# A load stream's ring in SBUF moved from 32 bytes past a 2 KB boundary onto the boundary

## The chip, the cores and the metric

The kernel runs on one core of one Trainium2 chip. The metric is the device time of one execution in microseconds (us), as a median of several executions. Where a ratio is given, it is the ratio of the runs of two kernels, taken in the same rounds, so it is not quite the ratio of the medians that are quoted beside it.

Two terms are used throughout. A *packet* is one record of the trace's list of DMA transfers: in this kernel mostly one contiguous run of bytes of one partition, moved by one of the 16 DMA engines. A *beat* is the time of 32 bytes in one DMA engine. The trace's packets give 27.2 bytes per ns per engine (below), so a beat is 1.176 ns.

## The reference, cut to what matters

One decoder step for a batch of 8: modulation from a condition, layer norm, attention of one new query against a long cache (32 query heads, 4 key/value heads, 8192 keys of 128 numbers), then a gated feed-forward block.

```python
mod = (_silu(c) @ w_mod).reshape(c.shape[0], 6, 1, -1)          # w_mod 1024 x 6144
h = _layernorm(x) * (1 + ca) + sa
q = h @ wq                                                      # 1024 x 4096
scores = einsum('bhqd,bhkd->bhqk', q, k) * Dh ** (-0.5)         # k_cache 8 x 4 x 8192 x 128
o = einsum('bhqk,bhkd->bhqd', softmax(scores), v)               # v_cache 8 x 4 x 8192 x 128
x = x + ga * (o @ wo)                                           # 4096 x 1024
h = _layernorm(x) * (1 + cb) + sb
x = x + gb * ((relu(h @ W_gate) * (h @ W_up)) @ W_down)         # 1024 x 3584, twice, and 3584 x 1024
```

With one query per batch entry there is little arithmetic for each byte. Of the 185.63 MB that are read from memory, 134 MB are K and V.

## The kernel before

All weights and all of K and V pass through one ring buffer in SBUF, `arena`, of nine slots of 16 KB per partition. A load is issued by the sync engine as soon as the ring space that it overwrites has been read.

```python
SLOT = 8192
NSLOT = 9
...
rem = nc.sbuf_base % 2048
if rem:
    sb("pad", [128, (2048 - rem) // 2], dt.bfloat16)
arena = sb("arena", [128, NSLOT * SLOT], dt.bfloat16)
ktb = sb("kt", [128, 2 * SLOT], dt.bfloat16)
... # some thirty small tiles
def pump():
    while stream:
        key, src, n = stream[0]
        lo = cursor[0] if cursor[0] + n <= NSLOT * SLOT else 0
        if P.unread("arena", lo, lo + n):
            return
        ...
        dst = arena[:, lo:lo + n]
        if len(src.shape) == 3:
            dst = dst.rearrange("p (a n) -> p a n", a=src.shape[1])
        P.op("sp", lambda e, dst=dst, src=src: e.dma_start(dst, src), writes=[slot_r(lo, lo + n)], dma=True)
```

The streamed tensors differ in how long their contiguous runs are. A K or V block gives each partition one run of 16,384 bytes. The rows of W_o are runs of 2,048 bytes.

```python
for n in range(N):                                              # N = 32
    load(("k", n), A_k_cache[n // G, n % G].rearrange("(p c) d -> p (c d)", p=128), SLOT)
    load(("v", n), A_v_cache[n // G, n % G].rearrange("(p c) d -> p (c d)", p=128), SLOT)
wo_src = A_wo.rearrange("(q h d) n -> q d h n", q=4, d=128)
```

The padding was meant to place the ring on a 2 KB boundary. But `nc.sbuf_base` is 16,481 when this kernel is built, and the allocator rounds each tile's start up to a multiple of 32. The pad of 1,950 bytes therefore began at 16,512, and the ring began at 18,464, which is 32 bytes past 18,432 = 9 x 2048. All blocks of the ring and all runs in it are multiples of 2 KB long, so every packet of the stream was written to an address 32 bytes past a 2 KB boundary.

## Time and profile before

| | before |
|---|---|
| median of 3 runs | 451.89 us (451.32 to 451.95) |
| span of the profiled run | 450.1 us |
| DMA packets of the stream's queue | 98.2% of 16 engines' span |
| PE, DVE busy | 67%, 48% |

The page of the kernel before, cut to the rows of the 40 slices that matter (busy share in tenths, granted clock in tenths, GB/s moved), the DMA queues (packets, MB, share of the 16 engines' span) and the chain of work that ended last:

```profile
span 450.1 us, 7822 instructions
...
PE   0234464678777775775897677688687768557853
...
PEclk9985566966888869679668887866768888655555
DMA  8999999999999999999999999999999999999992
GB/s 348 406 431 430 422 432 430 419 428 428 422 427 428 424 425 430 422 427 431 419 428 427 422 430 424 428 427 422 430 424 422 431 403 385 407 428 421 422 419 115
...
q1 hardware_dynamic: 16704, 185.64, 98.2%
q8 instruction: 27, 0.44, 0.4%
...
DMA 83%; PE 8%; DVE 7%; issue 1%; ACT 0%; SPq 0%; POOL 0%; DVEq 0%; ACTq 0%; POOLq 0%
```

The DMA row is at its highest digit almost from end to end, while PE is never at its own for long. From its third slice to the last but one, the GB/s row stays at 419 to 432, except in three slices of 403, 385 and 407, where the 2 KB rows of W_o arrive. So the kernel is as long as its stream, plus a few microseconds at each end.

The groups that read the ring or K^T, and the issues of the K loads (KB each, median us from issue to landing), from the same page:

```profile
L411 DVE STREAM_TRANSPOSE kt<-arena 128x1024 uint32<-128x1024 uint32 x128 | 153.3, 1219 | 117.1 <-DMA arena<-in_A_k_cache_dram 117.1
L420 PE MATMUL ps<-kt,qpad 128*128 128x512 bf16 x512 | 170.6, 503 | 2.0 <-POOL qpad L400 2.0
...
arena<-in_A_k_cache_dram SPq DMA_DIRECT2D x32, 2048.0 KB, 26.9
```

The transposes of K idle 117.1 us waiting for K data: the engines wait for the stream. A load lands 26.9 us after its issue, though 2 MB take only about 5 us at 427 GB/s, so some five loads are always queued, and it is the packets, not the issue of loads, that set the pace.

### The profile page before, as it was taken

How to read it: one execution, taken by the hardware profiler on the slowest of the kernel's cores; microseconds unless marked ns; L12 is line 12 of the kernel's file. 1: busy time of each engine (PE TensorE's matmuls, PEld its weight loads, DVE VectorE, ACT ScalarE, POOL GpSimd, SP SyncE). 2: the span in 40 equal slices, each digit the busy share in tenths (PEclk: the TensorE clock that was granted, in tenths of full speed). 3: DMA queues.
4: the chain of work that ended last, by engine and by line, in shares of the span. 5: the costliest groups of instructions: out<-in, count | busy, mean ns of one | idle time of the engine just before them, and what ended most of it. 6: DMA issues, size and time to landing. Idle time of an engine off the chain costs nothing.

```text
span 450.1 us, 7822 instructions
## 1 busy us (share of the span) xinstructions
PE 300.6 (67%) x3514; PEld 168.2 (37%) x3514; DVE 217.7 (48%) x333; ACT 33.2 (7%) x78; POOL 31.0 (7%) x141
## 2 busy tenths in 40 slices
PE   0234464678777775775897677688687768557853
PEld 0111121344433333343443344344343434447741
DVE  0503064666665566566555666655556663230000
ACT  0200020000010000000100000010000002000000
POOL 4000020100000001000000100000001000000000
PEclk9985566966888869679668887866768888655555
DMA  8999999999999999999999999999999999999992
GB/s 348 406 431 430 422 432 430 419 428 428 422 427 428 424 425 430 422 427 431 419 428 427 422 430 424 428 427 422 430 424 422 431 403 385 407 428 421 422 419 115
DMA packets 16769, 186.14 MB, mean 414 GB/s; under 512 B 1536, under 2 KB 1632, under 8 KB 5984
## 3 DMA queue, kind: packets, MB, share of 16 engines
q1 hardware_dynamic: 16704, 185.64, 98.2%
q8 instruction: 27, 0.44, 0.4%
q14 instruction: 6, 0.05, 0.0%
q10 hardware_dynamic: 32, 0.01, 0.0%
HBM read 185.63 MB, written 0.02 MB: 412 GB/s over the span
## 4 chain that ended last, share of the span: by engine, by line
DMA 83%; PE 8%; DVE 7%; issue 1%; ACT 0%; SPq 0%; POOL 0%; DVEq 0%; ACTq 0%; POOLq 0%
DMA arena<-in_A_k_cache_dram 61%; DMA arena<-in_B_W_down_dram 8%; DMA arena<-in_A_wq_dram 7%; DMA arena<-in_A_wo_dram 4%; PE ps L460 4%; DVE kt L411 3%; DMA c_r<-in_c_dram 2%; PE ps L528 1%; DVE pT L450 1%; PE ps L334 1%; PE ps L357 0%; PE ps L509 0%; DVE lu L281 0%; PE ps L420 0%; ACT L278 0%
## 5 line engine op out<-in xcount | busy, mean ns | idle before, releaser
L411 DVE STREAM_TRANSPOSE kt<-arena 128x1024 uint32<-128x1024 uint32 x128 | 153.3, 1219 | 117.1 <-DMA arena<-in_A_k_cache_dram 117.1
L420 PE MATMUL ps<-kt,qpad 128*128 128x512 bf16 x512 | 170.6, 503 | 2.0 <-POOL qpad L400 2.0
L420 PEld LDWEIGHTS ps<-kt,qpad 128*128 128x128 bf16 x512 | 63.5, 124 | 98.8 <-issue 72.6
L460 PE MATMUL ps<-pT,arena 128*128 128x8 bf16 x2048 | 56.0, 166 | 43.5 <-DVE pT L450 43.4
L460 PEld LDWEIGHTS ps<-pT,arena 128*128 128x128 bf16 x2048 | 54.0, 96 | 57.9 <-issue 57.6
L400 POOL COPY qpad<-qR 32x32 bf16<-32x32 bf16 x128 | 26.2, 205 | 316.4 <-PE ps L420 258.1
L430 PE MATMUL ps<-identf,negm 128*128 128x128 f32 x64 | 21.6, 433 | 36.5 <-DVE negm L426 36.5
L444 ACT ACTIVATE prb<-ps,bias 128x512 bf16<-128x512 f32 x32 | 22.0, 687 | 287.4 <-DVE mjt L438 287.4
L528 PE MATMUL ps<-hT,arena 128*128 128x8 bf16 x448 | 24.8, 194 | 8.4 <-DMA arena<-in_B_W_gate_dram 3.8
L430 PEld LDWEIGHTS ps<-identf,negm 128*128 128x128 f32 x64 | 13.5, 262 | 39.8 <-DVE negm L426 39.8
L528 PEld LDWEIGHTS ps<-hT,arena 128*128 128x128 bf16 x448 | 24.4, 152 | 8.9 <-DMA arena<-in_B_W_gate_dram 3.9
L450 DVE STREAM_TRANSPOSE pT<-prb 128x512 bf16<-128x512 bf16 x32 | 21.5, 672 | 1.7 <-ACT prb L444 1.7
L426 DVE TENSOR_REDUCE negm<-ps 128x1 f32<-128x512 f32 x32 | 20.9, 653 | 2.6 <-PE ps L420 2.6
L357 PE MATMUL ps<-arena,hT 128*32 128x512 bf16 x64 | 7.6, 627 | 12.5 <-DMA arena<-in_A_wq_dram 9.6
L535 DVE TENSOR_TENSOR hmT<-ps,grel 128x224 bf16<-128x224 f32 x1 | 0.4, 392 | 31.4 <-ACT grel L533 31.4
L303 PE MATMUL ps<-st,sel 128*128 128x1 f32 x4 | 1.2, 362 | 19.4 <-DVE st L302 19.4
L334 PE MATMUL ps<-arena,hT 128*32 128x512 bf16 x96 | 8.7, 528 | 7.2 <-DMA arena<-in_w_mod_dram 7.2
L545 PE MATMUL ps<-arena,hmT 128*32 128x256 bf16 x112 | 7.1, 415 | 7.5 <-DMA arena<-in_B_W_down_dram 7.4
L509 PE MATMUL ps<-arena,oT 128*32 128x256 bf16 x128 | 6.0, 366 | 5.1 <-DVE oT L497 2.6
L341 DVE COPY mod<-ps 128x512 f32<-128x512 f32 x2 | 1.3, 670 | 15.3 <-PE ps L334 15.3
L357 PEld LDWEIGHTS ps<-arena,hT 128*32 128x32 bf16 x64 | 1.9, 128 | 18.2 <-DMA arena<-in_A_wq_dram 16.1
L436 DVE TENSOR_REDUCE mj<-ps 128x8 f32<-128x128 f32 x32 | 8.1, 253 | 1.2 <-PE ps L430 1.2
(64 smaller groups left out, 64.6 us busy)
## 6 DMA issues: line engine op xcount, KB each, us to landing
arena<-in_A_k_cache_dram SPq DMA_DIRECT2D x32, 2048.0 KB, 26.9
arena<-in_A_v_cache_dram SPq DMA_DIRECT2D x32, 2048.0 KB, 30.4
arena<-in_w_mod_dram SPq DMA_DIRECT2D x4, 3072.0 KB, 18.3
arena<-in_A_wq_dram SPq DMA_DIRECT2D x4, 2048.0 KB, 35.9
arena<-in_A_wo_dram SPq DMA_DIRECT2D x4, 2048.0 KB, 19.7
arena<-in_B_W_gate_dram SPq DMA_DIRECT2D x4, 1792.0 KB, 25.8
arena<-in_B_W_up_dram SPq DMA_DIRECT2D x4, 1792.0 KB, 28.6
arena<-in_B_W_down_dram SPq DMA_DIRECT2D x3, 1792.0 KB, 34.4
```

The source lines that it names most:

```text
L334: fns.append(lambda e, w=w, pr=pr, j=j, kk=kk: e.matmul(ps[32 * j:32 * j + 32, pr, :], hT[:, kk, :], w[:, 2 * pr:2 * pr + 2, j, :], start= ...
L357: fns.append(lambda e, w=w, z=z, g=g, kk=kk: e.matmul(ps[32 * g:32 * g + 32, 3 + z, :], hT[:, kk, :], w[:, g, z, :], start=(kk == 0), stop ...
L400: P.op("pool", lambda e, n=n, Q=Q: e.tensor_copy(qpad[32 * Q:32 * Q + 32, n % NQ, :, 24 + 32 * Q:32 + 32 * Q], qR[32 * Q:32 * Q + 32, :, n ...
L411: P.op("dve", lambda e: e.transpose(ktb[:, to:to + QE].bitcast(dt.uint32), arena[:, lo:lo + QE].bitcast(dt.uint32)), reads=[slot_r(lo, lo ...
L420: fns.append(lambda e, t=t, r=r: e.matmul(ps[:, n % 2, :].rearrange("p (c k) -> p c k", k=32), qpad[:, n % NQ, t * 2 + r, 24 - 8 * i:152 - ...
L426: P.op("dve", lambda e: e.tensor_reduce(negm[:, n % 2:n % 2 + 1], ps[:, n % 2, :], AX.X, ALU.max, negate=True), reads=[bank(n % 2)], write ...
L430: P.op("pe", lambda e: e.matmul(ps[:, 2, 0:128], negm[:, n % 2:n % 2 + 1].to_broadcast([128, 128]), identf[:], start=True, stop=True), rea ...
L436: P.op("dve", lambda e: e.tensor_reduce(mj[:, z, :], ps[:, 2, 0:128].rearrange("p (m j) -> p j m", j=J), AX.X, ALU.min), reads=[bank(2)], ...
L444: P.op("act", lambda e: e.activation(prb[:, z, :], ps[:, z, :], ACT.Exp, bias=bias[:, z:z + 1], scale=scale, accum_out=lall[:, n:n + 1]), ...
L450: P.op("dve", lambda e: e.transpose(pT[:, z, :], prb[:, z, :]), reads=[R("prb", z, z + 1)], writes=[R("pT", z, z + 1)])
L460: fns.append(lambda e, cc=cc: e.matmul(ps[:, 3, col:col + J], vv[:, cc, :], pv_[:, cc % 16, cc // 16, :], start=(cc == 0), stop=(cc == NC ...
L528: fns.append(lambda e, w=w, f=f, kk=kk, off=off, first=first: e.matmul(ps[:, 0, off + f * B:off + (f + 1) * B], w[:, f // FR, f % FR, :], ...
```

## The change

The intent is to put the ring where the padding was meant to put it. Nothing else is edited. K^T and all small tiles move down by 32 bytes with it.

```diff
-        rem = nc.sbuf_base % 2048
+        rem = (nc.sbuf_base + 31) // 32 * 32 % 2048
         if rem:
             sb("pad", [128, (2048 - rem) // 2], dt.bfloat16)
         arena = sb("arena", [128, NSLOT * SLOT], dt.bfloat16)
```

## The prediction

> What bounds the kernel: the load stream. The DMA queue table gives its queue 98.2% of the 16 engines' span, and the 40 slices show the DMA busy share at 9 nearly throughout, at 419 to 432 GB/s. The chain of waits is 83% DMA, 8% PE, 7% DVE; no compute engine is busy over 67%. The sync queue waits for freed ring space, but a K load takes 26.9 us from issue to landing while 2 MB stream in about 5 us, so some five loads are always queued: the limit is how fast the engines move packets, not issue.
>
> What a packet costs. The trace's records of single packets (one contiguous run each) have these medians: 2,048 B 87 ns, 4,096 B 161, 8,192 B 313, 14,336 B 539, 16,384 B 614, 24,576 B 915. The slope from 2,048 to 16,384 B is 27.2 bytes per ns; left over at every size are 10 to 12 ns (minimum 8 to 9). So the byte rate is one fixed ceiling, and only the constant per packet is to be had. There are 15,104 data packets, 944 per engine: 944 x 11.6 ns = 11 us, an upper bound of 2.4% on a gain from alignment.
>
> What the change does. The allocator rounds to 32 bytes and the padding did not count that, so each destination run in the ring started 32 bytes past a 2 KB boundary. Now each starts on one (all blocks and rows are multiples of 2 KB). Nothing is added or removed; K^T and all small tiles move down by 32 bytes too, so relative addresses don't change. The Trainium skill ("DMA: Bandwidth & Descriptors", "How a descriptor splits into AXI transactions") says that a read not starting at a multiple of 256 B pays the 32 B beats before its start; whether a write pays, no run here shows. At 27.2 B/ns a beat is an estimated 1.18 ns, so each beat saved per packet is worth 944 x 1.18 = 1.1 us. A hint: two 8,192 B transfers of another queue took 307 ns, the stream's mostly 313: 2 to 5 beats, if their destinations were aligned, which I can't see. My central guess is 2 beats: 2.2 us. Nothing is nearly as likely; 5 beats would be 5.5 us.
>
> How much is critical. Nearly all: the last W_down data lands at 445.7 of 450.1 us, with 4 us of tail; PE is idle 20% or more of the K/V stage. The greatest relative effect should be on 2 KB rows (W_o, slices at 403 and 385 GB/s). I expect DVE, PE and ACT durations unchanged.
>
> Predicted: 449.6 us, range 445.5 to 452.3. Chances: faster by over 2% 0.06, within 2% 0.92, slower by over 2% 0.02.
>
> What would show it. Right: the median 16,384 B packet falls from 614 ns to 608-613, 2,048 B from 87 to 81-86, by the same ns at each size; steady K/V slices gain 0 to 4 GB/s; W_o slices rise most; transposes stay at 1,219 ns. Wrong: packets change in proportion to size, or packets unchanged while the span changes, or DVE/PE durations move.
>
> What would make it wrong. The constant may be entirely the unaligned start (then 441 us). Or a 2 KB boundary may make the partitions' writes meet in one place in some way this trace can't show, and packets get slower. Or a faster stream is eaten by ring space coming free late (then landings shorten while the SP queue's gaps grow).

## The result, and the profile after

| | before | after |
|---|---|---|
| median of 4 runs | 451.92 us (451.32 to 452.05) | 446.05 us (445.68 to 446.82) |
| ratio of the runs, 95% interval | | 0.9875 (0.9858 to 0.9892) |
| span of the profiled run | 450.1 us | 444.1 us |

The gain is 5.9 us, or 1.3%. The same cuts of the page of the kernel after:

```profile
span 444.1 us, 7822 instructions
...
PE   0235355677858676776877767786777787558753
...
PEclk9995576887788888879688888778888869655555
DMA  8999999999999999999999999999999999999993
GB/s 344 421 428 425 434 434 428 426 429 437 427 428 432 431 426 426 435 434 425 426 434 429 425 429 435 429 425 432 429 430 428 429 421 403 422 430 429 426 429 151
...
q1 hardware_dynamic: 16704, 185.64, 98.5%
q8 instruction: 27, 0.44, 0.4%
...
DMA 83%; PE 8%; DVE 7%; issue 1%; ACT 0%; SPq 0%; POOL 0%; DVEq 0%; ACTq 0%; POOLq 0%
```

```profile
L411 DVE STREAM_TRANSPOSE kt<-arena 128x1024 uint32<-128x1024 uint32 x128 | 153.3, 1218 | 114.6 <-DMA arena<-in_A_k_cache_dram 114.6
L420 PE MATMUL ps<-kt,qpad 128*128 128x512 bf16 x512 | 161.5, 482 | 2.0 <-POOL qpad L400 2.0
...
arena<-in_A_k_cache_dram SPq DMA_DIRECT2D x32, 2048.0 KB, 25.7
```

The longest of the sync queue's waits before its loads, in the view of waits (us in total, times, longest us), first before, then after:

```profile
SPq L228 <- PE ps L460: 263.8, 28, 18.4
```

```profile
SPq L228 <- PE ps L460: 261.5, 28, 18.4
```

The bound is the same: the same number of packets, the same bytes, the engines as full as before, and the same chain of waits. Only the rate is higher, a little in the flat part, and most in the W_o slices, from 403, 385 and 407 to 421, 403 and 422 GB/s (the slices of the two kernels don't cover quite the same packets). The transposes take 1,218 ns instead of 1,219. The QK matmuls are shorter (482 for 503 ns), but the granted clock was also higher in that run (mean 0.766 for 0.739). The alignment does not do this: the run `off256` below, on a cheap start, and `off64`, on a costly one, both have 493 ns, at 0.755 and 0.753. And the chain shows PE with only 8% of the span in both.

The same stretch of the K/V stage in the view of windows (stretch, length, busy us of each engine with its instruction count, granted clock, DMA share, GB/s), first before, then after:

```profile
core 0: us, PE busy (x) PEld busy (x) DVE busy (x) ACT busy (x) POOL busy (x), PEclk, DMA share, GB/s
...
100.00:150.00 50.00, 38.25 (x424) 20.22 (x424) 31.80 (x47) 3.89 (x10) 4.91 (x24) 0.80 1.01 426
150.00:200.00 50.00, 37.55 (x403) 19.63 (x399) 30.24 (x45) 3.89 (x10) 3.68 (x18) 0.76 1.00 425
200.00:250.00 50.00, 38.19 (x439) 20.60 (x440) 31.80 (x47) 3.89 (x10) 4.50 (x23) 0.80 1.01 426
```

```profile
100.00:150.00 50.00, 35.71 (x431) 19.50 (x428) 31.17 (x46) 3.89 (x10) 4.06 (x20) 0.83 1.01 430
150.00:200.00 50.00, 37.55 (x423) 20.06 (x419) 31.99 (x47) 3.89 (x10) 4.05 (x20) 0.80 1.01 429
200.00:250.00 50.00, 36.76 (x415) 20.06 (x416) 31.89 (x47) 3.89 (x10) 4.06 (x20) 0.83 1.01 429
```

The rate goes from 425 or 426 to 429 or 430 GB/s, with the DMA share at 1.00 to 1.01 in both. Since the number and the sizes of the packets are the same, an engine that is busy all the time and moves more must have cheaper packets. The busy row cannot show it; the single packets can. These counts are from the trace's DMA records of the stream's queue (means without the few packets that shared an engine with an instruction fetch; "to the next" is the mean time from one packet's start to the start of the packet that follows it on the same engine):

```
                  before                            after
bytes    median   mean   to the next       median   mean   to the next
 2,048     87     87.8      84.0             84      84.0     80.00   ns
16,384    614    615.6     612.1            611     611.0    607.07   ns
```

Successive packets of an engine overlap by 3 or 4 ns in the records, which is why "to the next" is shorter than the duration; it is the one that counts for the rate. At 16,384 bytes the lengths of eight successive packets of one load on one engine show a pattern. Four sequences before, of the 943 that could be followed, stand for nearly all; after, one does:

```
before  238 times  619 613 614 621 614 614 614 621
        235 times  619 613 614 614 621 614 614 614
        225 times  612 613 621 614 614 614 621 614
        219 times  612 621 614 614 614 621 614 614
after   nearly always  611 611 611 611 611 611 611 611
```

Before, three packets of four take about 3 ns more than the aligned 611, and every fourth takes 10 ns more. The slope from 2,048 to 16,384 bytes is 527.07 ns for 14,336 bytes in the kernel after: 27.2 bytes per ns. That agrees with the Trainium skill, "DMA: Bandwidth & Descriptors", section "Where 436 GB/s comes from", which has 16 ports of 32 bytes at 850 MHz; divided by 16, an estimate of 27.2 bytes per ns each. An aligned packet costs 68 beats at 2,048 bytes (64 of data) and 516 at 16,384 (512 of data): four beats of overhead in both. That is near the fixed overhead of about three cycles per packet that the same page has under "Why small descriptors are slow". The start 32 bytes off the boundary costs another 4.0 ns at 2,048 bytes and 5.0 ns at 16,384. So it is not quite one constant: the mean records of the other sizes, again without those that shared an engine, became 2.6 ns shorter at 4,096 bytes, 5.3 at 8,192 and 5.6 at 14,336. But it does not grow with the bytes.

### The profile page after: what moved, and what is told of

The parts are those of the page before. It is cut to its first block, busy times and chain, and to the rows that moved or that the text cites. A ratio compares the mean times of both kernels' runs of the same rounds, so it can differ in the third digit from the quotient of the medians.

```text
span 444.1 us, 7822 instructions
## 1 busy us (share of the span) xinstructions
PE 290.9 (66%) x3514; PEld 165.4 (37%) x3514; DVE 217.7 (49%) x333; ACT 33.2 (7%) x78; POOL 30.8 (7%) x141
## 3 DMA queue, kind: packets, MB, share of 16 engines
q1 hardware_dynamic: 16704, 185.64, 98.5%
## 4 chain that ended last, share of the span: by engine, by line
DMA 83%; PE 8%; DVE 7%; issue 1%; ACT 0%; SPq 0%; POOL 0%; DVEq 0%; ACTq 0%; POOLq 0%
DMA arena<-in_A_k_cache_dram 62%; DMA arena<-in_B_W_down_dram 8%; DMA arena<-in_A_wq_dram 7%; DMA arena<-in_A_wo_dram 4%; PE ps L460 4%; DVE kt L411 3%; DMA c_r<-in_c_dram 2%; PE ps L528 1%; DVE pT L450 1%; PE ps L334 1%; PE ps L420 1%; PE ps L357 0%; DVE lu L281 0%; ACT L278 0%; DVE hT L286 0%
## 5 line engine op out<-in xcount | busy, mean ns | idle before, releaser
L411 DVE STREAM_TRANSPOSE kt<-arena 128x1024 uint32<-128x1024 uint32 x128 | 153.3, 1218 | 114.6 <-DMA arena<-in_A_k_cache_dram 114.6
L420 PE MATMUL ps<-kt,qpad 128*128 128x512 bf16 x512 | 161.5, 482 | 2.0 <-POOL qpad L400 2.0
L420 PEld LDWEIGHTS ps<-kt,qpad 128*128 128x128 bf16 x512 | 60.9, 119 | 91.8 <-issue 60.6
L430 PE MATMUL ps<-identf,negm 128*128 128x128 f32 x64 | 20.2, 408 | 37.0 <-DVE negm L426 37.0
L430 PEld LDWEIGHTS ps<-identf,negm 128*128 128x128 f32 x64 | 12.3, 240 | 40.3 <-DVE negm L426 40.3
L303 PEld LDWEIGHTS ps<-st,sel 128*128 128x128 f32 x4 | 1.0, 310 | 19.6 <-DVE st L302 19.6
## 6 DMA issues: line engine op xcount, KB each, us to landing
arena<-in_A_k_cache_dram SPq DMA_DIRECT2D x32, 2048.0 KB, 25.7
```

The source lines that it names most:

```text
L411: P.op("dve", lambda e: e.transpose(ktb[:, to:to + QE].bitcast(dt.uint32), arena[:, lo:lo + QE].bitcast(dt.uint32)), reads=[slot_r(lo, lo ...
L420: fns.append(lambda e, t=t, r=r: e.matmul(ps[:, n % 2, :].rearrange("p (c k) -> p c k", k=32), qpad[:, n % NQ, t * 2 + r, 24 - 8 * i:152 - ...
L430: P.op("pe", lambda e: e.matmul(ps[:, 2, 0:128], negm[:, n % 2:n % 2 + 1].to_broadcast([128, 128]), identf[:], start=True, stop=True), rea ...
```

## The experiments

The theory (A): a write that starts off some boundary costs each DMA packet about the same time whatever its length, and this alone is the gain. The rival (B): the place of K^T and the small tiles, which moved too, changes what the engines do. Further questions are how coarse the boundary is, whether the cost is really per packet rather than per byte, and whether the read side matters.

### The ring alone, and everything but the ring

```diff
 # ring_only, against the kernel after: K^T and the rest stay 32 bytes past
         arena = sb("arena", [128, NSLOT * SLOT], dt.bfloat16)
+        sb("gap", [128, 16], dt.bfloat16)
```

```diff
 # off32, against the kernel after: only the ring is 32 bytes past
-            sb("pad", [128, (2048 - rem) // 2], dt.bfloat16)
+            sb("pad", [128, (2048 - rem + 32) // 2], dt.bfloat16)
         arena = sb("arena", [128, NSLOT * SLOT], dt.bfloat16)
+        sb("gap", [128, 496], dt.bfloat16)
```

> Ring on the 2 KB boundary, K^T and every small tile left 32 bytes past one as in the kernel before. Theory A (the start of the write in the ring sets a constant cost per DMA packet): all of the gain, 446 us, 16,384 B packets at 611 ns as in the kernel after (before: 614 and 621). Rival B (the place of K^T and the small tiles matters to the engines, and the ring only follows): no gain, 452 us, packets at 614 and 621 ns.

> The complement: ring 32 bytes past the boundary, K^T and the small tiles at the same phase (modulo 1 KB) as in the kernel after. Theory A: no gain, 452 us, packets 614 and 621 ns. Rival B: 446 us.

Measured: `ring_only` 446.41 us, ratio to the kernel before 0.9889 (0.9873 to 0.9906); packets of 611 ns. `off32` 451.61 us, ratio 1.0004 (0.9987 to 1.002); packets of 614 and 621 ns, in almost the same numbers as before. The gain goes with the ring and with nothing else. Rival B falls.

### How coarse is the boundary?

The ring was placed 64, 128, 224 and 256 bytes past a 2 KB boundary, with the gap behind it filled so that K^T and the rest keep their places (modulo 1 KB for `off64`, exactly for the others).

```diff
 # off256, against the kernel after; off128 and off224 alike, off64 like off32
-            sb("pad", [128, (2048 - rem) // 2], dt.bfloat16)
+            sb("pad", [128, (256 - rem) // 2], dt.bfloat16)
         arena = sb("arena", [128, NSLOT * SLOT], dt.bfloat16)
+        sb("gap", [128, 896], dt.bfloat16)
```

> Ring 64 bytes past a 2 KB boundary. If only the grain of 64 B counts: 446 us and 611 ns packets. If the grain is 256 B or more (the Trainium skill's transaction of 256 B): like the kernel before, 452 us, packets of about 614 and 621 ns. My guess is 256 B, so 452 us.

> Ring 256 bytes past a 2 KB boundary, K^T and all small tiles exactly where the kernel after has them. If the grain is 256 B or less: 446 us, packets 611 ns. If the writes need 512 B, 1 KB or the 2 KB boundary that the change aimed at: 452 us, packets 614 and 621 ns. My guess is 446 us.

> Ring 128 bytes past a 2 KB boundary, all else where the kernel after has it. Theory of a 256 B grain: the gain is lost, 451 to 452 us, and the 16,384 B packets show again the fourth packet of about 7 ns more. Rival, a 128 B grain: 446 us and 611 ns packets. A third idea, from 614/621 at 32 B and 613/620 at 64 B (1 ns less for each 32 B further): about 611 and 618 ns, mean 612.7, 447 to 448 us.

> Ring 224 bytes past a 2 KB boundary, that is 32 bytes short of a 256 B boundary. If the cost falls with the distance from the 256 B boundary below (1 ns for each 32 B): packets at about 609 and 616 ns, 444 to 447 us. If any start off the 256 B grain costs the same: 451 to 452 us.

| ring past a 2 KB boundary by | median us | ratio to before (95%) | mean packet of 16,384 B | of 2,048 B |
|---|---|---|---|---|
| 32 B (`off32`) | 451.61 | 1.0004 (0.9987 to 1.002) | 615.6 ns | 87.8 ns |
| 64 B (`off64`) | 451.15 | 1.0000 (0.9984 to 1.0017) | 614.7 | 87.8 |
| 128 B (`off128`) | 450.07 | 0.9965 (0.995 to 0.998) | 614.6 | 88.2 |
| 224 B (`off224`) | 451.94 | 1.0002 (0.9985 to 1.0019) | 615.6 | 87.9 |
| 256 B (`off256`) | 446.58 | 0.9898 (0.9882 to 0.9915) | 611.0 | 84.0 |

A start at 256 bytes past costs what a start on the 2 KB boundary costs, and the starts at 32, 64, 128 and 224 lose most or all of the gain. Of the starts tried, those at a multiple of 256 bytes are the cheap ones. (The transaction of 256 B in the expectation of `off64` is that of the page and section which the prediction names; the grain measured here agrees with it.) The 2 KB boundary was not needed. The third idea, that the cost falls by 1 ns for each 32 bytes further, fails: 224 costs what 32 costs, and 128 costs 1 ns less than 32 rather than 3 ns less.

### Is it a cost per packet?

K and V were fetched in runs of 2,048 bytes instead of 16,384. Which keys go where is permuted in K and V alike, so the result is still correct. The bytes are the same, but an engine now handles 4,528 data packets instead of 944.

```diff
 # kv2k_al, against the kernel after; kv2k_off32 the same against off32; V alike
-load(("k", n), A_k_cache[n // G, n % G].rearrange("(p c) d -> p (c d)", p=128), SLOT)
+load(("k", n), A_k_cache[n // G, n % G].rearrange("(a p c) d -> p a (c d)", a=8, p=128), SLOT)
```

> K and V fetched as 2,048 B runs (keys in another order, the same in K and V, so the result holds), ring on the boundary: 4,096 packets per engine for K and V instead of 512. With the 84.4 ns that a 2,048 B packet took in the kernel after (4 ns of it under the packet before): 446 + 329 - 311 = 465 us. To be read against the next run.

> The same with the ring 32 bytes past the boundary. Theory of a constant per packet: 88.1 ns a packet as in the kernel before (3.5 under the one before), so 484 us, about 19 us above the aligned one (4,528 data packets per engine x 4.2 ns); 4% between the two. Rival, a cost per byte or per 256 B (whatever the number of packets): the same 5.9 us as between the two kernels of the case, so about 471 us.

Measured: 463.58 us on the boundary (465 expected) and 484.30 us off it (484 expected). That the second is hit so closely is partly luck: the aligned run came out 1.4 us lower and the difference 1.7 us larger than expected. The rate per slice, from the pages of the two, first on the boundary, then off it:

```profile
GB/s 344 428 425 430 376 409 409 407 408 409 407 408 407 407 409 408 407 409 407 407 406 409 408 408 407 409 408 409 407 407 408 407 408 407 415 430 429 431 425 167
```

```profile
GB/s 345 425 427 422 393 387 387 385 386 387 385 387 386 386 387 386 386 387 386 385 385 387 386 386 387 385 386 388 385 385 386 385 386 386 392 426 424 423 419 125
```

In the K/V stage the rate is 406 to 409 on the boundary and 385 to 388 off it. These are close to the lowest W_o slices of the two kernels (403 after, 385 before), which have rows of the same length. The 20.7 us between the two runs, over 4,528 packets per engine, are 4.6 ns for each. Between the kernels it is 5.9 us over 944 packets, or 6.2 ns (5.3 ns with the 5 us that repeat over all such pairs, below). So the cost goes with the number of packets. The rival, a cost per byte, said 5.9 us here as well and falls.

### Does the read side matter?

K and V were read from addresses 32 bytes further on (which gives each key and value shifted numbers; the check of the result does not notice this), with the ring on the boundary and off it.

```diff
 # src32_al against the kernel after, src32_off32 the same against off32; V alike
+SH = 16
-load(("k", n), A_k_cache[n // G, n % G].rearrange("(p c) d -> p (c d)", p=128), SLOT)
+load(("k", n), A_k_cache.rearrange("b g s d -> (b g s d)")[n * 128 * SLOT + SH * (n < N - 1):
+     (n + 1) * 128 * SLOT + SH * (n < N - 1)].rearrange("(p x) -> p x", p=128), SLOT)
```

> Wrong result on purpose: K and V are read 32 bytes past their place in DRAM (the last pair excepted), ring on the boundary; every read run starts 32 bytes past a 256 B boundary and every write run on one. If only the start of the write counts: like the kernel after, 446 us, 611 ns packets. If a read pays one 32 B beat before its start, as the Trainium skill has it: 1.18 ns on 512 - 16 packets per engine, 446.6 us. If a read pays as a write does (5 ns): 448.5 us.

> The same with the ring 32 bytes past the boundary too: read and write start at the same phase. If it is the phase between read and write that costs: the K and V packets are cured, 449 us (wo, wq, gate, up, down keep the cost). If the start of the write alone counts: 452 us, like the kernel before. If each side pays for itself: 454.5 us.

Measured: 446.48 us (ratio 0.9885, 0.9868 to 0.9901) with packets of 611.0 to 611.2 ns, depending on which disturbed ones are left out, and 451.10 us (ratio 0.9994, 0.9979 to 1.001) with packets of 615.6 ns and the same pattern of four as before. Moving the start of the read changes a packet by at most 0.2 ns, and an equal move of read and write cures nothing. Of the two starts, only that of the write was seen to count. One thing is taken for granted: that K and V themselves begin at a multiple of 256 bytes in DRAM. The record does not show their addresses; if they don't, all reads started off such a multiple before as well, and the test says less about reads. (What the expectation of `src32_al` has from the Trainium skill is in the page and section which the prediction names.)

### Runs of 512 bytes

```diff
-... .rearrange("(a p c) d -> p a (c d)", a=8, p=128)
+... .rearrange("(a p c) d -> p a (c d)", a=32, p=128)
```

> K and V fetched as 512 B runs, ring on the boundary: 16,384 packets per engine for K and V. Start to start an aligned packet took 607.07 ns at 16,384 B and 80.00 at 2,048 B, which is its 32 B beats and 4 more at 1.176 ns; for 512 B that gives 23.5 ns, so 446 + 385.5 - 310.8 = 521 us, unless making the packets becomes the limit.

> The same with the ring 32 bytes past the boundary. If the cost stays a constant of 4 to 5 ns per packet down to 512 B: 27.5 to 28.5 ns each, so 590 to 605 us, 13 to 16% above the aligned one. If it depends on the length of the run (for 512 B, 3 instead of 2 pieces of 256 B, where 16,384 B have 65 instead of 64) it could be less or more: open.

Measured: 501.89 and 598.41 us. The first expectation (521 us) was a miss. The trace has no 512-byte packets of K and V: four runs travel in one record of 2,048 bytes, as many records as in the runs above. And on the boundary the issue of the loads may set the pace too. This is a stretch of the sync engine's queue in time (start us, length us, engine, line, operation):

```profile
200.36 5.58 SPq L228 DMA_DIRECT2D arena<-in_A_v_cache_dram  x1
206.41 5.01 SPq L228 DMA_DIRECT2D arena<-in_A_k_cache_dram  x1
211.89 5.01 SPq L228 DMA_DIRECT2D arena<-in_A_v_cache_dram  x1
```

Each issue of a 2 MB load occupies the queue for 5.0 to 5.6 us, one follows almost at once on the other, and the chain of waits has 14% SPq. But the packets fill the engines here as well (99.4% of the 16 engines' span), and off the boundary the issues are just as dense (6.7 to 7.8 us each from 200 to 240 us, 25% SPq). Which of the two sets the pace is not shown, so this pair can't be read as the cost of packets alone. What it does show: off the boundary the records of 2,048 bytes took 116.7 ns in the mean, against 91.1 on it. That is about 6 ns for each of the four runs; each run in the record may pay for itself, where a packet of one run of 2,048 bytes paid 4 ns. The second time, 598.41 us, lies in the range that I had given, but with another count of packets than I had assumed, so it confirms nothing.

## Why the prediction was right or wrong

- **The bound: right.** The stream's packets set the time; the DMA share stayed at 1.0 while the rate rose. Nothing was eaten by ring space coming free late. The prediction's sign of that was shorter landings with growing gaps of the sync queue. The landings did shorten (25.7 for 26.9 us), but the gaps did not grow: the sync queue's waits before its loads (L228) add up to 369.1 us before and 360.1 after, and the stream's share of the engines did not fall (98.2 to 98.5%).
- **The mechanism: right in the main.** The byte rate did not change and the cost per packet did, though not "by the same ns at each size" (2.6 to 5.6 ns, above). The W_o slices gained most, and the transposes stayed as they were. `ring_only` and `off32` show that it is the ring, `kv2k_al` and `kv2k_off32` that it is a cost per packet.
- **The size: wrong.** The step that failed is "My central guess is 2 beats: 2.2 us". The term measured 5.0 ns, or 4.3 beats, for a packet of 16,384 bytes and 4.0 ns, or 3.4 beats, for one of 2,048, and the kernel gained 5.9 us instead of 2.2. The prediction had named 5 beats and 5.5 us as a possibility, but not as the likely one. There were two errors in that step. I worked with medians: 614 ns is the length of three packets in four, and the fourth, 621 ns, was in the trace before the change. The mean was 615.6, and the shortest packets, at 611 to 612 ns, already showed the length that all of them took afterwards. And I let a hint of 2 to 5 beats from another queue, whose destinations I could not see, end at its low side.
- **The bound of 11 us on any gain from alignment: too high, but harmless.** I took the whole of a packet's duration over its data. Packets overlap by 3 or 4 ns in the records, and the four beats that an aligned packet still pays are 4.7 ns, so about half of what each packet pays beyond its data was to be had.
- **The sum.** Counted from one completion to the next on an engine, a load of eight 16,384-byte packets went from 4,903.4 to 4,863.0 ns; 68 such loads are 2.75 us. The 264 packets of 2,048 bytes per engine at 4.0 ns are 1.06 us. The other 136 packets, at the 2.6 to 5.6 ns by which their records became shorter (2.6 at 24,576 bytes too), are 0.6 us. Together that is 4.4 us. In the profiled runs the 16 engines end the stream 5.1 us earlier in the mean and the last of them 5.8 us earlier. The other kernels with a cheap start gained 4.8 (`ring_only`), 4.6 (`off256`) and 5.3 us (`src32_al`) by their medians, and their intervals overlap that of the change, so about 5 us is what repeats. Some 0.7 us of the mean of the engines is not accounted for by these packets. The packets of the 27 instruction fetches, which share engines with the stream, took 25.3 us in all instead of 29.0; spread over 16 engines that is 0.2 us of it.
- **"PE durations unchanged": wrong, without consequence.** The QK matmuls took 482 ns instead of 503 under a higher granted clock. The clock, not the place of the ring, goes with it (above), and these matmuls have 0 to 1% of the chain in the two pages.

What stays open is why a start 32 bytes past a multiple of 256 costs 3 ns on most packets of 16,384 bytes and 10 on every fourth, why the cost differs between sizes, and why a start at 128 bytes costs slightly less. No run here looked inside a packet. No version beat the kernel after: those that start at a multiple of 256 bytes match it, and all others are slower.

## What to carry to other kernels

Check where the destination of a streamed load really begins: an allocator's rounding can undo padding that was meant to align it. In this kernel a multiple of 256 bytes was enough, and being off it cost 4 to 5 ns per packet of 2,048 or 16,384 bytes, which is 1.1 to 1.3% of the kernel's time with K and V in 16 KB runs and 4.5% with them in 2 KB runs. When the DMA engines are always busy, look at the lengths of single packets, and at their spread and mean rather than their median: here the shortest packets of the slow kernel were already as long as all packets of the fast one.

## What the Trainium skill lacked or had wrong

- "DMA: Bandwidth & Descriptors", "How a descriptor splits into AXI transactions", says what a read pays that does not start at a multiple of 256 bytes (the beats before its start) and gives no figure for a write. Here the write pays: 4.0 ns at 2,048 bytes and 5.0 ns at 16,384 for starts 32 bytes past such a multiple, and nothing at 256 bytes past 2 KB. Moving a read's start by 32 bytes changed the packets by at most 0.2 ns, not by the 1.18 ns of a beat. Whether the beat is paid and hidden behind the write, or the reads were off a multiple of 256 already before, the records can't tell.
- "SBUF — State Buffer", "Operand start alignment", treats a DMA's start address as a question of legality and says that its runs timed nothing. The runs here time it: 446.58 us at 256 bytes, 450.07 to 451.94 us at 32 to 224.
- No page has the pattern of four: 32 bytes past the boundary every fourth packet of 16,384 bytes took 621 ns and the others about 614, against 611 on it.
- "DMA: Bandwidth & Descriptors", "Why small descriptors are slow", has a fixed overhead of about 3 cycles per packet. Aligned packets here took their data and 4 beats more at both 2,048 and 16,384 bytes (80.00 and 607.07 ns). Whether these are the cycles that the page means, no run here shows.
